# Top-k attention into a Sinkhorn mixture of experts: order of weight conversions, output copies and block boarding

## The chip, the cores and the metric

One core of one Trainium2 chip. The metric is the device time of one execution in microseconds (us). TensorE (PE in the profile) multiplies, VectorE (DVE), ScalarE (ACT) and GpSimd (POOL) do the rest, and the queue of SyncE (SP) issues the transfers.

## The reference

Attention over 4 batches of 8 heads, 576 tokens, head size 64, in which each query keeps only its 32 highest scores; its output, 2304 tokens of 512 features, goes through 8 dense experts whose outputs are summed with weights that a Sinkhorn iteration balances.

```python
def _attn_ref(q, k, v):                       # q, k, v: (4, 8, 576, 64)
    scores = scale * np.matmul(q, k.transpose(0, 1, 3, 2))
    kth = np.partition(scores, -top_k, axis=-1)[..., -top_k:-top_k + 1]   # top_k = 32
    scores = np.where(scores >= kth, scores, -1000000000.0)
    attn = np.exp(scores - np.max(scores, axis=-1, keepdims=True))
    attn = attn / (np.sum(attn, axis=-1, keepdims=True) + 1e-09)
    return np.matmul(attn, v)

def _moe_ref(x, w_gate, w1, w2):              # x: (2304, 512), w1: (8, 512, 1024), w2: (8, 1024, 512)
    logits = x @ w_gate
    P = np.exp(logits - logits.max())
    for _ in range(8):
        P /= P.sum(1, keepdims=True) + 1e-09
        P /= P.sum(0, keepdims=True) + 1e-09
        P *= N / E
    for e in range(E):
        h = np.maximum(x @ w1[e], 0.0)
        out += P[:, e:e + 1] * (h @ w2[e])
```

## The kernel before, in words

**Precision.** Most products are made from a high and a low part of each factor (`wh`, `wl` of a weight; `xh`, `xl` of the tokens; `hh`, `hl` of the hidden layer), as three matmuls. Splitting a weight tile of 128 x 1024 is a *conversion*: a transfer into `wr` (3 buffers), ACT's copy to `wh` (line 81, `hi_act`) and POOL's subtraction to `wl` (line 87, `lo_pool`), with 6 buffers each for `wh` and `wl`.

**Attention.** It runs in seven stages; a stage is a batch and one or two phases of 256 queries. A phase goes through four head pairs. For each score tile PE multiplies (lines 122 and 123, 4 matmuls), ACT copies (`s`, line 131, 3 buffers), and DVE finds the 32 highest by four MAX (line 142) and three MATCH_REPLACE (line 147) passes over 576 columns. ACT makes the exponentials and scales them, PE transposes (line 239, 9 transposes for two score tiles), ACT and DVE (or POOL, `evac_pool`, in the very first phase) split the result, PE multiplies by v (lines 252 and 253), and DVE adds the two halves into `xt` (line 256), a quarter of it for each head pair. Where both halves exist the four head pairs give `xt`, 256 tokens ("a block").

**Visits.** The MoE hides under the attention. Blocks 0, 1, 2, 3 and 5 are *boarded* into two seats of 256 columns: ACT and DVE split `xt` into the seat's `xh` and `xl` (lines 367 and 368). Then turn v, a call of `visit`, takes expert v mod 8 to every block that is seated, and a block leaves after 8 turns. The table `BOARD` names the turn at which a block boards; there are 24 turns. In a turn the hidden layer comes first (line 424, into p1), then `store_hidden` (lines 473 and 474), then the second product (line 511), whose result ACT copies to `y` (line 519) for a transfer to memory. If both seats are taken (and neither by block 0), one matmul of 512 columns serves both; a block alone has matmuls of 256 columns.

Block 0 is special. `first_half` multiplies its first two quarters with half of every expert's `w1` in plain float32 while the last two head pairs are still in work (lines 454, 457, 459: matmul, copy, transfer to memory); the visit adds the stored half (line 469) and needs only the other half of `w1`, so a turn with block 0 alone converts 6 tiles and others 8.

**The rest.** The four blocks that never board are multiplied at the end by one level of Strassen's scheme (`hidden_pair`, `last_outputs`), from factors that ACT and POOL make when the attention is over.

**What sets the order.** Each engine runs its instructions in a fixed order. A scheduler sets it when the program is built: of what is ready in its own reckoning, the highest priority goes first. Attention stages have priority BIG, `store_hidden` 2 BIG, `first_half` -BIG, everything else of a visit none. Attention stages are emitted when their `xt` buffers (3) are free, which hangs on `BOARD`.

Of the kernel before, what the change touches and what calls it, by code (L numbers as in the profile page):

```python
# [9 lines left out]
AF = mybir.ActivationFunctionType  # L10
# [4 lines left out]
DM, E, F = 512, 8, 1024  # L15
N = NB * S
NT = N // 128
KD = DM // 128
# [14 lines left out]
BLOCKS.append([("m", 0, 1), ("m", 2, 3)])  # L33


BOARD = {0: 0, 1: 4, 2: 8, 3: 12, 5: 16}
SEAT = {0: 0, 1: 1, 2: 0, 3: 1, 5: 0}


# [10 lines left out]
def kernel(  # L50
# [11 lines left out]
    nc = tc.nc  # L62
    BIG = 1000000
# [237 lines left out]
    def attend_stage(b, phases, mix):  # L301
        xts = {}
        for ph in phases:
            xts[ph] = xp.tile([128, KD, 256], F32, name="xt", bufs=XR)
            for t in range(2):
                X["t", b, 2 * ph + t] = xts[ph][:, :, t * 128:(t + 1) * 128]
        xm = None
        if mix:
            m = ("m", b // 2 * 2, b // 2 * 2 + 1)
            if m not in X:  # L310
                X[m] = xp.tile([128, KD, 128], F32, name="xm", bufs=2)
                mixed[m] = 0
            xm = X[m][:, :, (b % 2) * 64:(b % 2) * 64 + 64]
            mixed[m] += 1
        for hp in range(HP):
            if (b, phases, hp) == (0, (0,), 2):
                with tc.high_priority(offset=-BIG):
                    first_half(xts[0])
            attend_heads(b, hp, phases, xts, xm)
        for ph in phases:  # L320
            t = tile_id["t", b, 2 * ph]
            if 2 * b + ph == PARKED:
                nc.sync.dma_start(parked, xts[ph])
            gate_logits(xts[ph], [t, t + 1])
        if mix and mixed[m] == 2:
            gate_logits(X[m], [tile_id[m]])
# [77 lines left out]
    def convert(src, shape):  # L404
        wr = wp.tile(shape, F32, name="wr", bufs=WR)
        nc.sync.dma_start(wr, src)
        return split_weights(wr, shape)

    def split_weights(wr, shape):
        wh = wp.tile(shape, F32R, name="wh", bufs=WB)  # L410
        wl = wp.tile(shape, F32R, name="wl", bufs=WB)
        hi_act(wh, wr)
        lo_pool(wl, wr, wh)
        return wh, wl
# [13 lines left out]
    def hidden(seat, n, s, wh, wl):  # L428
        m = 512 // n
        for f0 in range(0, 2, m):  # L430
            ps = ps1.tile([128, m, n], F32, name="p1")
            products(ps, f0, seat, n, wh, wl, 0)
            with tc.high_priority(offset=2 * BIG):
                store_hidden(seat, slice(2 * s + f0, 2 * s + f0 + m), slice(seat.c0, seat.c0 + n), ps)
# [5 lines left out]
    def half_weights(e, s2, half):  # L440
        wr = wp.tile([128, 2, 2, 256], F32, name="wr", bufs=WR)
        for r in range(2):
            nc.sync.dma_start(wr[:, r], w1[e, 2 * s2 + r, :, 2 * half:2 * half + 2, :])
        return wr

    def first_half(x):
        for e in range(E):
            for s2 in range(2):
                wr = half_weights(e, s2, 0)
                for r in range(2):  # L450
                    ps = ps1.tile([128, 2, 256], F32, name="p1")
                    for fo in range(2):
                        for kk in range(2):
                            nc.tensor.matmul(ps[:, fo, :], wr[:, r, kk, fo * 128:(fo + 1) * 128], x[:, kk, :],  # L454
                                             start=(kk == 0), stop=(kk == 1))
                    y = op_.tile([128, 512], F32, name="y", bufs=YB)
                    nc.scalar.activation(y, ps.rearrange("p a b -> p (a b)"), AF.Copy)
                    PART[e, 2 * s2 + r] = dram.tile([128, 512], F32, name=f"p{e}_{s2}_{r}")
                    nc.sync.dma_start(PART[e, 2 * s2 + r], y)

    def second_half(e, s, seat, wh, wl, k0):
        y = op_.tile([128, 512], F32, name="y", bufs=YB)
        nc.sync.dma_start(y, PART[e, s])
        y = y.rearrange("p (a b) -> p a b", a=2)
        ps = ps1.tile([128, 2, 256], F32, name="p1")
        products(ps, 0, seat, 256, wh, wl, k0)
        ft = slice(2 * s, 2 * s + 2)
        with tc.high_priority(offset=2 * BIG):
            nc.vector.tensor_tensor(ps, ps, y, op=OP.add)
            store_hidden(seat, ft, slice(0, 256), ps)  # L470

    def store_hidden(seat, ft, cs, src):
        nc.scalar.activation(seat.hh[:, ft, cs], src, AF.Relu)  # L473
        nc.vector.scalar_tensor_tensor(seat.hl[:, ft, cs], src, 0.0, seat.hh[:, ft, cs].bitcast(F32),  # L474
                                       op0=OP.max, op1=OP.subtract)

    def visit(v, on):
        e = v % E
        ids = [SEAT[blk] for blk in on]
        groups = []  # L480
        if on[0] == 0:
            on_first, ids = True, ids[1:]
        else:
            on_first = False
        if 0 in ids and 1 in ids:
            groups, ids = [(seats[0], 512)], [i for i in ids if i > 1]
        groups += [(seats[i], 256) for i in ids]
        if groups:
            for s in range(4):
                wh, wl = convert(w1[e, s], [128, KD, 256])  # L490
                if on_first:
                    second_half(e, s, seats[0], wh[:, 2:4], wl[:, 2:4], 2)
                for seat, n in groups:
                    hidden(seat, n, s, wh, wl)
        else:
            for s2 in range(2):
                wr = half_weights(e, s2, 1)
                wh, wl = split_weights(wr, [128, 2, 2, 256])
                for r in range(2):
                    second_half(e, 2 * s2 + r, seats[0], wh[:, r], wl[:, r], 2)  # L500
        ws = [convert(w2[e, s], [128, 2, 512]) for s in range(4)]
        for blk in on:
            seat = seats[SEAT[blk]]
            for ti, piece in enumerate(BLOCKS[blk]):
                ts = slice(seat.c0 + ti * 128, seat.c0 + (ti + 1) * 128)
                ps = ps2.tile([128, 512], F32, name="p2")
                i = 0
                for ft in range(NFT):
                    wh, wl = ws[ft // 2]
                    for a, m in ((seat.hh, wh), (seat.hh, wl), (seat.hl, wh)):  # L510
                        nc.tensor.matmul(ps, a[:, ft, ts], m[:, ft % 2, :],  # L511
                                         start=(i == 0), stop=(i == 3 * NFT - 1))
                        i += 1
                output(v, tile_id[piece], ps)

    def output(v, t, ps):
        e = v % E
        y = op_.tile([128, 512], F32, name="y", bufs=YB)
        nc.scalar.activation(y, ps, AF.Copy)
        spill[t, e] = dram.tile([128, 512], F32, name=f"y{t}_{e}")  # L520
        nc.sync.dma_start(spill[t, e], y)

# [264 lines left out]
```

## Time and profile before

| | |
|---|---|
| median of 3 runs | 1947.8 us (1945.65 to 1948.59) |
| profiled execution, its own time | 1946.94 us |
| its span in the trace | 1945.2 us |
| PE busy | 1874.1 us, 96% |
| DVE busy | 1351.9 us, 70% |
| ACT busy | 1145.8 us, 59% |
| POOL busy | 1057.5 us, 54% |
| TensorE clock granted, mean | 0.989 |

The span is the time from the first to the last instruction that the trace holds; 1.7 us of the execution lie around it. Busy shares are means over stages with different limits: until about 476 us DVE is busy nearly all the time, from there PE is. All times below are from this one execution.

### The profile page before, as it was taken

How to read it: one execution, taken by the hardware profiler on the slowest of the kernel's cores; microseconds unless marked ns; L12 is line 12 of the kernel's file. 1: busy time of each engine (PE TensorE's matmuls, PEld its weight loads, DVE VectorE, ACT ScalarE, POOL GpSimd, SP SyncE). 2: the span in 40 equal slices, each digit the busy share in tenths (PEclk: the TensorE clock that was granted, in tenths of full speed). 3: DMA queues.
4: the chain of work that ended last, by engine and by line, in shares of the span. 5: the costliest groups of instructions: out<-in, count | busy, mean ns of one | idle time of the engine just before them, and what ended most of it. 6: DMA issues, size and time to landing. Idle time of an engine off the chain costs nothing.

```text
span 1945.2 us, 27297 instructions
## 1 busy us (share of the span) xinstructions
PE 1874.1 (96%) x9617; PEld 1590.8 (82%) x9617; DVE 1351.9 (70%) x2620; ACT 1145.8 (59%) x1993; POOL 1057.5 (54%) x914
## 2 busy tenths in 40 slices
PE   4799889999999999999999999999999999999998
PEld 3688788998888888888888888888888888888886
DVE  8979999999988998469998823135555555543333
ACT  6978877777777787568777754543333333333331
POOL 4548866645645445464444478864545544555440
PEclk9899989999999999999999999999999999999999
DMA  3477654434434324343333325633333333311211
GB/s 117 135 240 263 212 173 159 141 123 148 127 118 129 111 89 143 119 153 119 99 113 111 98 87 174 206 129 98 103 113 114 105 113 103 92 60 55 65 33 43
DMA packets 96073, 240.02 MB, mean 123 GB/s; under 512 B 10816, under 2 KB 12992, under 8 KB 95936
## 3 DMA queue, kind: packets, MB, share of 16 engines
q1 hardware_dynamic: 95936, 238.28, 38.4%
q8 instruction: 75, 1.23, 0.3%
q14 instruction: 62, 0.51, 0.1%
HBM read 203.64 MB, written 34.60 MB: 122 GB/s over the span
## 4 chain that ended last, share of the span: by engine, by line
PE 82%; DVE 12%; DMA 2%; ACT 1%; issue 1%; POOL 1%; SPq 0%; ACTq 0%; POOLq 0%; DVEq 0%
PE p L511 18%; PE p L681 18%; PE p L424 18%; PE p L622 9%; DVE m L142 5%; PE pc L622 5%; DVE w L147 4%; PE pb L622 2%; PE pt L239 2%; PE p L454 2%; PE sp L123 2%; PE sp L122 2%; PE pt L252 2%; PE pt L253 2%; DVE hl L474 1%
## 5 line engine op out<-in xcount | busy, mean ns | idle before, releaser
L87 POOL TENSOR_TENSOR wl<-wr,wh 128x1024 fp32r<-128x1024 f32 x280 | 675.7, 2424 | 520.0 <-ACT wh L81 504.1
L81 ACT ACTIVATE wh<-wr 128x1024 fp32r<-128x1024 f32 x280 | 296.2, 1060 | 297.8 <-PE p L622 194.4
L142 DVE MAX8 m<-w 128x8 f32<-128x576 f32 x432 | 318.6, 749 | 2.9
L424 PE MATMUL p<-xh,wh 128*128 128x256 f32 (+1 forms) x768 | 263.6, 343 | 6.7 <-DVE hl L474 6.7
L424 PE MATMUL p<-xl,wh 128*128 128x256 f32 (+1 forms) x768 | 261.4, 341 | 1.7 <-DVE xl L90 1.7
L424 PE MATMUL p<-xh,wl 128*128 128x256 f32 (+1 forms) x768 | 262.1, 342 | 0.0
L511 PE MATMUL p<-wh,hh 128*128 128x512 f32 x640 | 253.1, 400 | 2.1 <-ACT hh L473 2.0
L511 PE MATMUL p<-wl,hh 128*128 128x512 f32 x640 | 251.9, 396 | 0.0
L511 PE MATMUL p<-wh,hl 128*128 128x512 f32 x640 | 245.8, 395 | 0.0
L147 DVE MATCH_REPLACE8 w<-m,w 128x576 f32<-128x576 f32 x288 | 213.3, 741 | 0.1
L528 DVE SCALAR_TENSOR_TENSOR acc<-p,P,acc 128x512 f32<-128x512 f32 x120 | 89.5, 750 | 166.8 <-PE p L681 166.8
L681 PE MATMUL p<-wh,h2h 128*128 128x512 f32 x512 | 200.0, 391 | 1.3 <-ACT h2h L645 0.7
L681 PE MATMUL p<-wl,h2h 128*128 128x512 f32 x512 | 199.9, 390 | 0.0
L681 PE MATMUL p<-wh,h2l 128*128 128x512 f32 x512 | 196.7, 390 | 0.0
L474 DVE SCALAR_TENSOR_TENSOR hl<-p,hh 128x512 fp32r<-128x512 f32 x160 | 109.0, 682 | 100.0 <-ACT hh L473 99.0
L424 PEld LDWEIGHTS p<-xh,wh 128*128 128x128 f32 x768 | 146.7, 191 | 23.1 <-DVE hl L474 7.2
L424 PEld LDWEIGHTS p<-xl,wh 128*128 128x128 f32 x768 | 146.8, 191 | 16.9 <-DVE xl L90 2.0
L424 PEld LDWEIGHTS p<-xh,wl 128*128 128x128 f32 x768 | 146.7, 191 | 14.1
L142 DVE MAX8 m<-s 128x8 f32<-128x576 f32 x144 | 107.9, 749 | 50.6 <-ACT s L131 25.8
L511 PEld LDWEIGHTS p<-wh,hh 128*128 128x128 f32 x640 | 121.3, 190 | 23.2 <-ACT hh L473 2.4
L511 PEld LDWEIGHTS p<-wl,hh 128*128 128x128 f32 x640 | 121.5, 190 | 21.8
L511 PEld LDWEIGHTS p<-wh,hl 128*128 128x128 f32 x640 | 120.6, 189 | 22.6
(175 smaller groups left out, 4079.9 us busy)
## 6 DMA issues: line engine op xcount, KB each, us to landing
wr<-in_w_dram SPq DMA_DIRECT2D x240, 512.0 KB, 3.5
y<-y SPq DMA_DIRECT2D x160, 256.0 KB, 2.7
raw<-in_k_dram SPq DMA_DIRECT2D x56, 288.0 KB, 3.0
wr<-in_w_dram SPq DMA_DIRECT2D x48, 256.0 KB, 3.7
raw<-in_q_dram SPq DMA_DIRECT2D x32, 256.0 KB, 3.2
p<-y SPq DMA_DIRECT2D x32, 256.0 KB, 3.4
y<-p SPq DMA_DIRECT2D x32, 256.0 KB, 4.4
raw<-in_v_dram SPq DMA_DIRECT2D x28, 288.0 KB, 3.4
```

Of the source, the lines that this page charges most:

```text
L81: nc.scalar.activation(dst, src, AF.Copy)
L87: nc.gpsimd.tensor_tensor(dst, src, hi.bitcast(F32), op=OP.subtract)
L122: nc.tensor.matmul(o, qc, kh[:, cs], start=(i == 0), stop=False)
L123: nc.tensor.matmul(o, qc, kl[:, cs], start=False, stop=(i == n - 1))
L142: nc.vector.max(m8[:, u, r, :], ws[u] if r else units[u][0])
L147: nc.vector.match_replace(ws[u], m8[:, u, r, :], ws[u] if r else units[u][0], LOWEST)
L424: nc.tensor.matmul(ps[:, fo, :], a[:, kk, fs], x[:, k0 + kk, cs], start=(i == 0), stop=(i == 3 * nk - 1))
L474: nc.vector.scalar_tensor_tensor(seat.hl[:, ft, cs], src, 0.0, seat.hh[:, ft, cs].bitcast(F32), op0=OP.max, op1=OP.subtract)
L511: nc.tensor.matmul(ps, a[:, ft, ts], m[:, ft % 2, :], start=(i == 0), stop=(i == 3 * NFT - 1))
L528: return nc.vector.scalar_tensor_tensor(ACC[t], y, g, ACC[t], op0=OP.mult, op1=OP.add)
L622: nc.tensor.matmul(ps, w[:, kk, :], x[:, kk, :], start=(fresh and i == 0), stop=(i == 5), skip_group_check=True)
L681: nc.tensor.matmul(ps, a[:, ft, ts], m[:, ft, :], start=(i == 0), stop=(i == 11))
```

## The change

Three things. `BOARD` moves block 1 from turn 4 to turn 6 and block 3 from turn 12 to turn 14; the number of turns stays 24. The conversions of a visit are taken out of its loop into `visit_weights` and given priority 2 BIG, above attention, and so is the copy of an output (`y`, now line 530). And the conversions of the very first visit (two halves of `w1`, four tiles of `w2`) are called in stage one ahead of `first_half`, instead of at the visit.

```diff
--- before.py
+++ after.py
@@ -33,7 +33,7 @@
 BLOCKS.append([("m", 0, 1), ("m", 2, 3)])
 
 
-BOARD = {0: 0, 1: 4, 2: 8, 3: 12, 5: 16}
+BOARD = {0: 0, 1: 6, 2: 8, 3: 14, 5: 16}
 SEAT = {0: 0, 1: 1, 2: 0, 3: 1, 5: 0}
 
 
@@ -315,6 +315,7 @@
         for hp in range(HP):
             if (b, phases, hp) == (0, (0,), 2):
                 with tc.high_priority(offset=-BIG):
+                    ready[0] = visit_weights(0, True)
                     first_half(xts[0])
             attend_heads(b, hp, phases, xts, xm)
         for ph in phases:
@@ -474,6 +475,19 @@
         nc.vector.scalar_tensor_tensor(seat.hl[:, ft, cs], src, 0.0, seat.hh[:, ft, cs].bitcast(F32),
                                        op0=OP.max, op1=OP.subtract)
 
+    ready = {}
+
+    def visit_weights(v, alone):
+        e = v % E
+        if alone:
+            w1s = []
+            for s2 in range(2):
+                wh, wl = split_weights(half_weights(e, s2, 1), [128, 2, 2, 256])
+                w1s += [(wh[:, r], wl[:, r]) for r in range(2)]
+        else:
+            w1s = [convert(w1[e, s], [128, KD, 256]) for s in range(4)]
+        return w1s, [convert(w2[e, s], [128, 2, 512]) for s in range(4)]
+
     def visit(v, on):
         e = v % E
         ids = [SEAT[blk] for blk in on]
@@ -485,20 +499,16 @@
         if 0 in ids and 1 in ids:
             groups, ids = [(seats[0], 512)], [i for i in ids if i > 1]
         groups += [(seats[i], 256) for i in ids]
-        if groups:
-            for s in range(4):
-                wh, wl = convert(w1[e, s], [128, KD, 256])
-                if on_first:
-                    second_half(e, s, seats[0], wh[:, 2:4], wl[:, 2:4], 2)
-                for seat, n in groups:
-                    hidden(seat, n, s, wh, wl)
-        else:
-            for s2 in range(2):
-                wr = half_weights(e, s2, 1)
-                wh, wl = split_weights(wr, [128, 2, 2, 256])
-                for r in range(2):
-                    second_half(e, 2 * s2 + r, seats[0], wh[:, r], wl[:, r], 2)
-        ws = [convert(w2[e, s], [128, 2, 512]) for s in range(4)]
+        if v not in ready:
+            with tc.high_priority(offset=2 * BIG):
+                ready[v] = visit_weights(v, not groups)
+        w1s, ws = ready.pop(v)
+        for s, (wh, wl) in enumerate(w1s):
+            if on_first:
+                k0 = 2 if groups else 0
+                second_half(e, s, seats[0], wh[:, k0:k0 + 2], wl[:, k0:k0 + 2], 2)
+            for seat, n in groups:
+                hidden(seat, n, s, wh, wl)
         for blk in on:
             seat = seats[SEAT[blk]]
             for ti, piece in enumerate(BLOCKS[blk]):
@@ -516,7 +526,8 @@
     def output(v, t, ps):
         e = v % E
         y = op_.tile([128, 512], F32, name="y", bufs=YB)
-        nc.scalar.activation(y, ps, AF.Copy)
+        with tc.high_priority(offset=2 * BIG):
+            nc.scalar.activation(y, ps, AF.Copy)
         spill[t, e] = dram.tile([128, 512], F32, name=f"y{t}_{e}")
         nc.sync.dma_start(spill[t, e], y)
```

**Start of the program, ACT.** The rows are ACT's from its first splits of q and k on, before; `s` is the copy of a score tile, names with numbers are buffers.

```order
L81 ACTIVATE qs_105<-raw_103 128x512
L81 ACTIVATE kh_110<-raw_108 128x576
L81 ACTIVATE kh_116<-raw_114 128x576
L131 ACTIVATE s_139<-sp_134 128x576
L131 ACTIVATE s_146<-sp_141 128x576
L81 ACTIVATE qs_299<-raw_297 128x512
L81 ACTIVATE kh_304<-raw_302 128x576
L131 ACTIVATE s_208<-sp_203 128x576
L81 ACTIVATE kh_310<-raw_308 128x576
```

The same place of ACT in the changed kernel.

```order
L81 ACTIVATE qs_105<-raw_103 128x512
L81 ACTIVATE kh_110<-raw_108 128x576
L81 ACTIVATE kh_116<-raw_114 128x576
L81 ACTIVATE wh_494<-wr_491 128x1024
L131 ACTIVATE s_139<-sp_134 128x576
L81 ACTIVATE qs_299<-raw_297 128x512
L131 ACTIVATE s_146<-sp_141 128x576
L81 ACTIVATE wh_501<-wr_498 128x1024
L81 ACTIVATE kh_304<-raw_302 128x576
L131 ACTIVATE s_208<-sp_203 128x576
L81 ACTIVATE wh_507<-wr_505 128x1024
L81 ACTIVATE wh_513<-wr_511 128x1024
```

Six conversions (`wh`) of the first visit now stand among the first attention instructions, the first of them ahead of the first copy of scores; before, they stood after the 24th to 27th copy of scores.

**Second head pair of the first phase, DVE.** The rows are DVE's around the two additions that complete the second quarter of block 0's `xt` (`pt_465`, `pt_478`), which `first_half` needs; before.

```order
L142 MAX m8_1068<-s_1064 128x8
L147 MATCH_REPLACE w_1066<-m8_1068,w_1066 128x576
L148 SCALAR_TENSOR_TENSOR eb_945<-m8_943,nb_944 128x2
L256 TENSOR_TENSOR xt_102<-pt_465,tmp_464 64x256
L147 MATCH_REPLACE w_1067<-m8_1068,s_1064 128x576
L142 MAX m8_1068<-w_1066 128x8
L256 TENSOR_TENSOR xt_102<-pt_478,tmp_464 64x256
L142 MAX m8_1137<-s_1126 128x8
L142 MAX m8_1068<-w_1067 128x8
```

The same two additions in the changed kernel.

```order
L147 MATCH_REPLACE w_1173<-m8_1175,s_1164 128x576
L156 RECIPROCAL st_964<-st_964 128x2
L142 MAX m8_1106<-w_1105 128x8
L142 MAX m8_1175<-w_1173 128x8
L256 TENSOR_TENSOR xt_102<-pt_465,tmp_464 64x256
L256 TENSOR_TENSOR xt_102<-pt_478,tmp_464 64x256
L147 MATCH_REPLACE w_1105<-m8_1106,w_1105 128x576
L147 MATCH_REPLACE w_1173<-m8_1175,w_1173 128x576
```

Ahead of the second of them stood 52 MAX and 39 MATCH_REPLACE of DVE's order; now 57 and 42 do.

## Rows read from the trace of the kernel before

**Rows 1.** Busy time by stretch: length, busy (count) per engine, PEclk, DMA share, GB/s.

```profile
core 0: us, PE busy (x) PEld busy (x) DVE busy (x) ACT busy (x) POOL busy (x), PEclk, DMA share, GB/s
0.00:50.00 50.00, 22.52 (x75) 17.01 (x76) 44.47 (x93) 32.22 (x58) 21.11 (x34) 1.00 0.37 113
50.00:77.70 27.70, 18.12 (x78) 14.53 (x78) 27.54 (x60) 24.36 (x50) 18.01 (x30) 0.82 0.19 53
77.70:157.50 79.80, 75.59 (x406) 66.57 (x405) 63.25 (x137) 65.63 (x132) 35.40 (x48) 0.98 0.75 246
157.50:209.00 51.50, 47.74 (x304) 42.28 (x302) 50.39 (x102) 44.85 (x77) 49.00 (x42) 1.00 0.75 253
209.00:265.00 56.00, 48.28 (x275) 42.78 (x276) 55.03 (x106) 45.92 (x84) 43.13 (x40) 0.88 0.64 200
265.00:476.00 211.00, 201.64 (x1324) 184.47 (x1323) 205.04 (x433) 163.57 (x301) 122.85 (x131) 0.98 0.46 148
476.00:1276.00 800.00, 797.18 (x4287) 683.00 (x4287) 593.68 (x1263) 549.88 (x981) 451.30 (x379) 1.00 0.39 124
1276.00:1945.20 669.20, 663.08 (x2880) 540.13 (x2878) 312.50 (x432) 219.32 (x317) 316.66 (x214) 1.00 0.28 88
```

**Rows 2.** Timeline of PE: start us, length, operation, [idle before <-what ended it].

```profile
77.31 0.55 PE L239 MATMUL pt<-idt,Et 128*128 128x128 f32 x3 [0.77 <-DVE xt L256]
77.70 2.75 PE L454 MATMUL p<-xt,wr 128*128 128x256 f32 x12
...
152.26 2.88 PE L454 MATMUL p<-xt,wr 128*128 128x256 f32 x8 [2.75 <-ACT y L457]
...
265.12 0.28 PE L424 MATMUL p<-xh,wh 128*128 128x256 f32 x1
...
476.27 0.39 PE L424 MATMUL p<-xh,wh 128*128 128x512 f32 x1
```

**Rows 3.** Timeline of ACT, two places.

```profile
6.79 0.65 ACT L131 ACTIVATE s<-sp 128x576 f32<-128x576 f32 x1 [0.89 <-PE sp L123]
...
150.66 1.06 ACT L81 ACTIVATE wh<-wr 128x1024 fp32r<-128x1024 f32 x1 [2.75 <-DMA wr<-in_w_dram]
```

**Rows 4.** Timeline of DVE, three places.

```profile
101.17 0.74 DVE L142 MAX8 m<-w 128x8 f32<-128x576 f32 x1
101.83 0.07 DVE L147 MATCH_VALUE_LOAD w<-m,s 128x8 f32 x1
...
102.55 0.07 DVE L147 MATCH_VALUE_LOAD w<-m,w 128x8 f32 x1
...
117.35 0.76 DVE L142 MAX8 m<-s 128x8 f32<-128x576 f32 x1 [7.55 <-ACT s L131]
...
152.62 0.56 DVE L90 TENSOR_TENSOR atl<-pt,ath 128x384 fp32r<-128x384 f32 x1 [2.65 <-ACT ath L81]
```

**Rows 5.** The chain that ended last, in order of time: start us, us, what.

```profile
510.33 2.73 PE p L424 x12
...
1194.07 2.88 PE p L424 x24
```

**Rows 6.** The page's costliest groups: operation xcount | busy, mean ns | idle before.

```profile
L87 POOL TENSOR_TENSOR wl<-wr,wh 128x1024 fp32r<-128x1024 f32 x280 | 675.7, 2424 | 520.0 <-ACT wh L81 504.1
```

**Rows 7.** Groups of DVE between 265 and 476 us.

```profile
L474 DVE SCALAR_TENSOR_TENSOR hl<-p,hh 128x512 fp32r<-128x512 f32 x33 | 22.5, 680 | 2.1 <-ACT hh L473 2.0
...
L469 DVE TENSOR_TENSOR p<-p,y 128x512 f32<-128x512 f32 x16 | 11.0, 688 | 0.5 <-PE p L424 0.4
```

**Rows 8.** Line 148: duration ns min/median/max, first and last start us.

```profile
L148 DVE SCALAR_TENSOR_TENSOR eb<-m,nb x80: 132/230/2396, 22.5 to 1111.5; 128x2 f32<-128x2 f32 x64, 128x1 f32<-128x1 f32 x16
```

**Rows 9.** Timeline of the SP queue at the start.

```profile
3.07 0.91 SPq L443 DMA_DIRECT2D wr<-in_w_dram  x2
```

**Rows 10.** The page's transfers: xcount, KB each, median us from issue to landing.

```profile
wr<-in_w_dram SPq DMA_DIRECT2D x48, 256.0 KB, 3.7
```

**Rows 11.** Timelines of DVE and POOL: the last addition of attention, the last Strassen factor.

```profile
1143.66 0.22 DVE L258 TENSOR_TENSOR xm<-pt,tmp 64x64 f32<-64x64 f32 x1
...
1176.54 2.46 POOL L87 TENSOR_TENSOR T4l<-tf,T4h 128x1024 fp32r<-128x1024 f32 x1
```

## The prediction

> **What bounds the kernel now.** I read the busy time by stretch first, because a mean over the span hides that the limit changes. From 1276.0 us on the last four blocks run, PE is busy 663.08 of 669.20 us, and the change touches nothing there [rows 1]. From 476 to 1276 PE is busy 797.18 of 800 us: work taken from PE there is worth its full length, and a shorter wait of another engine is worth nothing. From 0 to 77.7 and from 157.5 to 476 DVE is busy nearly all the time (27.54 of 27.70, 50.39 of 51.50, 55.03 of 56.00, 205.04 of 211.00), while PE idles 27.5, 9.6, 3.8, 7.7 and 9.4 us in the five stretches; these are attention's stretches, whose length DVE's top-k passes set. Between 77.7 and 157.5 it is the other way round: PE works off `first_half`, idles 4.2 us, and DVE idles 16.6 us.
>
> Then the timelines, for what ended the idle times. `first_half` gets going at 77.70, right behind a DVE addition into `xt` [rows 2]. It ends late because of one wait: ACT stood 2.75 us for the transfer of a weight tile of the first visit [rows 3], the copy of PE's result stood behind it, and PE waited 2.75 us until 152.26 [rows 2]. DVE's two clear holes in the stretch, 7.55 and 2.65 us, end with ACT too [rows 4].
>
> **Part 1, boarding.** Turns 4 and 5 lose block 1 and turns 20 and 21 have two blocks instead of one, so paired turns go from 12 to 14. A hidden layer is 96 matmuls: 384 of 256 columns become 192 of 512. In the chain, 12 of 512 columns took 2.73 us and 24 of 256 took 2.88 us [rows 5], 0.228 and 0.120 each: 46.1 us become 43.8, 2.3 less. Half of it falls behind 476 us, where PE is the limit: **-1.1**. The other half is in part 2. Two more turns with block 0 alone mean four conversions fewer, at 2.42 us of POOL each [rows 6]. Behind 476 us POOL works 451 of 800 us [rows 1], so that is hidden; it would be worth 9.7 us at most if POOL were the limit.
>
> **Part 2, what the early turns now hold.** I counted PE's whole order. When turn 4 begins, both kernels have issued 147 transposes; before, 282 at the start of turn 8; changed, 246 at the start of turn 8 and the same 282 at the start of turn 9. So the same attention and (but for 1.2 us) the same visits lie between, distributed differently. Before, that took 265.12 to 476.27, 211.2 us [rows 2], with 205.0 us of DVE, of which visits have 22.5 + 11.0 = 33.5 [rows 7]: attention 171.5 for 135 transposes, 1.27 each. PE had 201.6, of it visits 4 x (144 x 0.120 + 96 x 0.228) = 156.7: attention 44.9, 0.333 each. Changed, up to turn 8: DVE 99 x 1.27 + 27.3 (two turns of 4 additions and 4 stores, two with 4 more stores) = 153.1, at DVE's present share of 97% 157.5; PE 33.0 + 33.4 + 78.3 = 144.7. DVE is the limit: 157.5. Turn 8: PE 43.8 + 36 x 0.333 = 55.8, DVE 51.1. PE is the limit. Together 213.3: **+2.1**. The work is the same but no longer evenly spread, which is where the small loss is from. From below 0 (the waits are filled), from above 6 (the 9.4 us that PE idles now are lost on top in equal share).
>
> **Part 3, the first visit's conversions in stage one.** Removed: ACT's wait of 2.75 us and with it PE's, **-2.75**; from below 0, since another copy may stand behind a transfer, from above 4.2, all that PE idled in the stretch. Added is work in the first 40 us: six conversions, 6 x 1.06 us of ACT [rows 3] and 6 x 2.42 = 14.5 us of POOL. ACT does 32.2 and POOL 21.1 of 50 us there [rows 1], so there is room; but what queues behind them is the chain that DVE lives on. Two steps. First, a `wh` now stands ahead of the first copy of scores. Its two transfers are issued from 3.07 us on [rows 9], the second some 0.48 later, and need 3.7 us [rows 10]: it starts at 7.2 and the copy, at 6.79 before [rows 3], at about 8.2: 1.4 us later, and all of DVE's top-k with it. Second, five MAX and three MATCH_REPLACE more stand ahead of the addition that `first_half` waits for. On DVE one MAX lasts 0.66 us from start to start and one MATCH_REPLACE with its load 0.72 [rows 4]: 5 x 0.66 + 3 x 0.72 = 5.5 us. DVE has no hole there to make that up. `first_half` gets going 6.9 us later, and everything behind it: **+6.9**. From below 1.4 (if the additions wait for their matmuls anyway and DVE's other holes shrink), from above 11.4, with two small DVE instructions blocked as follows.
>
> Line 148 is a DVE instruction on two columns. Its shortest took 132 ns, its longest 2396 [rows 8], about one POOL subtraction of 2424 ns [rows 6]. The Trainium skill, "SBUF - State Buffer", section "Who interferes with whom", says that a DVE instruction with both inputs in SBUF contends with a GpSimd instruction that reads SBUF, and that whoever issues first holds the shared pair for its whole length. The trace agrees with that length. By that rule alone each of the two or three such DVE instructions that meet the moved subtractions would cost up to 2.3 us, and none elsewhere; by the rows I take 0 for the likeliest and 2 x 2.3 for the upper bound, since the median is 230 ns.
>
> Between 157.5 and 209 POOL is busy 49.0 of 51.5 us [rows 1]; 14.5 us of that now lie earlier. DVE's holes from there to 265 are only 2.1 us, and the excess of line 148 is hidden in its busy time (0.23 less 0.13 us at the median, some 17 of them). I take **-1.2**, bounds 0 and -6.
>
> **Part 4, priority.** From turn 1 on the conversions stand between the same copies of scores as before, to within one or two, since they wait for one of six buffers anyway. PE waits nowhere by name for the output copy. So 0 here, and what hides a conversion is DVE's stock of three copied score tiles. If that cover is gone, the rival below is the price.
>
> **Sum.** -1.1 + 2.1 - 2.75 + 6.9 - 1.2 = +3.95. The profiled execution took 1946.94 us (span 1945.2 and 1.7 around it), 0.9 below the runs' median: **1950.9 us**.
>
> **Rivals.**
> 1. *Faster: DVE's holes close.* The first visit no longer disturbs ACT, and an earlier q load ends the wait of 7.55 us; then DVE, the limit from 157.5 to 476, has 7.55 + 2.65 us more. For it: both holes end with ACT, and ACT's own wait causes the second. Against it: PE's order gives out score tiles at the same pace, with `first_half` between them. With the late start made good (+6.9 becomes 0, the wait is inside the 10.2): 1946.9 - 1.1 + 2.1 - 10.2 - 1.2 = 1936.5. It decides from the point where the first visit's line 424 begins before 154 us.
> 2. *Slower: conversions starve attention.* Between 157.5 and turn 8 stand 46 conversions; where their `wh` or `wl` goes ahead of a small instruction that DVE waits for, it costs up to 1.06 or 2.42 us. At a quarter of the 1.06 each, 12 us: 1962.9. For it: DVE is the limit there, and ACT serves DVE in order. Against it: the conversions' places hardly moved. It decides from the point where DVE's share between 157.5 and turn 8 falls below 95%.
> 3. *Slower at the end.* Block 3's later boarding holds back the last attention stage, and the Strassen factors are late. Now the last addition is at 1143.66, the last factor at 1178.8 [rows 11], 97 us ahead of their use at 1276. Even two paired turns (2 x 43.8 us) would not use that up; if it did with 15 us on top, 1966.
>
> The Trainium skill would have rival 2 by way of the same shared pair: under the rule named above a higher priority for POOL's subtractions means more of them in flight when line 148 comes. No row tells the two ways apart.
>
> **How the numbers follow.** The likeliest case, 46 in 100, is the sum: 1944 to 1957 with its bounds. Rival 1 has 28, rival 2 21, rival 3 5. The range 1937 to 1963 leaves out some of rival 1, rival 3 and the outer part of rival 2. About 3.9 us (0.2%) is what a measurement can tell from no change. Faster than 1943.9: nearly all of rival 1 and a little of the likeliest, 0.30. Slower than 1951.7: rivals 2 and 3 and a quarter of the likeliest, 0.38. The rest 0.32.
>
> **What would show it.** The first MAX near 8.9 instead of 7.47 us; `first_half` going on near 84 us instead of 77.7; no wait of line 454 over 1 us; the first visit near 161 us instead of 157.5; turn 8 near 425 us, with PE idle some 13 us in the 160 before; PE without gaps from there; the last stretch 669 us as now. The prediction is wrong if DVE idles much less than 16 us ahead of the first visit, or much more than 3% behind it.

## The result, and the profile after

The changed kernel took 1969.9 us (median, 1967.65 to 1973.63), the kernel before 1946.7 in the same comparison: a ratio of 1.012, interval 1.0102 to 1.0139, 23 us slower. The forecast was 1950.9 with a range up to 1963. The profiled execution has a span of 1965.9 us against 1945.2 [rows 1], 20.7 longer; the account below is of these two.

The changed kernel by stretch, cut where its own stages begin: until `first_half` goes on, until the first visit, until turn 4, until turn 8, until turn 9, until the last visit's end, to the end (columns as in [rows 1]).

```profile
0.00:87.90 87.90, 41.74 (x150) 32.91 (x151) 78.97 (x167) 64.13 (x116) 54.45 (x71) 0.91 0.39 117
87.90:166.30 78.40, 76.10 (x406) 66.85 (x405) 55.43 (x120) 61.97 (x127) 29.93 (x45) 0.97 0.75 243
166.30:281.60 115.30, 99.36 (x588) 88.16 (x587) 113.21 (x217) 90.14 (x158) 83.63 (x79) 0.93 0.59 191
281.60:446.00 164.40, 146.59 (x937) 132.38 (x936) 159.64 (x316) 126.86 (x231) 101.06 (x103) 0.96 0.49 159
446.00:499.90 53.90, 53.90 (x279) 45.89 (x278) 52.54 (x109) 40.71 (x76) 30.57 (x30) 1.00 0.39 128
499.90:1296.60 796.70, 794.80 (x4195) 677.43 (x4195) 598.90 (x1264) 537.49 (x968) 428.63 (x369) 1.00 0.37 119
1296.60:1965.90 669.30, 663.17 (x2880) 540.16 (x2879) 313.28 (x432) 220.35 (x318) 319.67 (x215) 1.00 0.28 88
```

Read the lengths against those of before (77.7, 79.8, 107.6, 211.2 to the start of turn 8, which has the same attention behind it as turn 9 now, 799.7, 669.2): **+10.2, -1.4, +7.7, +7.1, -3.0, +0.1**, together the 20.7 by which the spans differ. All of the loss lies ahead of 500 us, where DVE sets the pace but for the stretch of `first_half`. DVE's idle time there is length less busy: 30.3 us before [rows 1], now 8.9 + 23.0 + 2.1 + 4.8 + 1.4 = 40.1. So 9.8 of the 23.6 us by which turn 9 is late are idle time of DVE, and 13.8 are busy time.

What the busy time is, two lines of DVE show: their groups up to turn 8 of the kernel before (xcount | busy, mean ns),

```profile
L148 DVE SCALAR_TENSOR_TENSOR eb<-m,nb 128x2 f32<-128x2 f32 x31 | 17.2, 556 | 0.1
L90 DVE TENSOR_TENSOR xl<-xt,xh 128x256 fp32r<-128x256 f32 x12 | 9.2, 769 | 0.0
L148 DVE SCALAR_TENSOR_TENSOR eb<-m,nb 128x1 f32<-128x1 f32 x3 | 0.7, 223 | 0.0
```

and up to turn 9 of the changed kernel:

```profile
L148 DVE SCALAR_TENSOR_TENSOR eb<-m,nb 128x2 f32<-128x2 f32 x31 | 27.7, 895 | 0.1
L90 DVE TENSOR_TENSOR xl<-xt,xh 128x256 fp32r<-128x256 f32 x12 | 10.7, 896 | 0.0
L148 DVE SCALAR_TENSOR_TENSOR eb<-m,nb 128x1 f32<-128x1 f32 x3 | 1.3, 428 | 0.1
```

The same 46 instructions take 39.7 us instead of 27.1: 12.6 of the 13.8. They do no more work; they are held, and by POOL's subtractions. In each kernel 17 of these 34 instructions of line 148 last over 0.33 us, and each of these 17 ends within 0.03 us of the end of a subtraction of line 87. It is not a wait for `nb`, which POOL makes for line 148 as well: each `nb` had been ready for at least 3.9 us. What the change altered is which subtraction they met: that of a weight (`wl`, the longest) 5 times before, 11 times now. DVE's timeline at two of the held instructions,

```profile
208.70 2.37 DVE L148 SCALAR_TENSOR_TENSOR eb<-m,nb 128x2 f32<-128x2 f32 x1
...
338.45 4.95 DVE L90 TENSOR_TENSOR xl<-xt,xh 128x256 fp32r<-128x256 f32 x1
```

and POOL's at the same places:

```profile
208.37 2.69 POOL L87 TENSOR_TENSOR wl<-wr,wh 128x1024 fp32r<-128x1024 f32 x1 [1.51 <-ACT wh L81]
...
338.34 1.02 POOL L87 TENSOR_TENSOR vz<-raw,vz 64x64 fp32r<-64x64 f32 x2
339.32 2.40 POOL L87 TENSOR_TENSOR wl<-wr,wh 128x1024 fp32r<-128x1024 f32 x1
341.68 1.43 POOL L87 TENSOR_TENSOR kl<-raw,kh 128x576 fp32r<-128x576 f32 x1
343.19 0.39 POOL L87 TENSOR_TENSOR vz<-raw,vz 64x64 fp32r<-64x64 f32 x1
```

The first DVE instruction ends at 211.07 us, POOL's subtraction at 211.06. The second ends at 343.40, 0.3 us behind the last of four subtractions that followed each other without a pause (338.34 to 343.11); that it got in only at POOL's pause is read from these times. The Trainium skill, "SBUF — State Buffer", section "Who interferes with whom", says that a DVE instruction with both inputs in SBUF contends with a GpSimd instruction that reads SBUF. The trace agrees, with 2.37 us for an instruction whose shortest is 132 ns [rows 8].

The start of the loss is in stage one. ACT's timeline, and DVE's (the first MAX, the second addition into `xt`, the longest hole):

```profile
7.71 1.06 ACT L81 ACTIVATE wh<-wr 128x1024 fp32r<-128x1024 f32 x1 [0.95 <-DMA wr<-in_w_dram]
8.67 0.63 ACT L131 ACTIVATE s<-sp 128x576 f32<-128x576 f32 x1
...
84.52 0.68 ACT L81 ACTIVATE kh<-raw 128x576 fp32r<-128x576 f32 x1 [1.88 <-DMA raw<-in_k_dram]
85.23 0.78 ACT L255 ACTIVATE tmp<-pt 64x256 f32<-64x256 f32 x2
```

```profile
9.33 0.76 DVE L142 MAX8 m<-s 128x8 f32<-128x576 f32 x1 [1.79 <-ACT s L131]
...
86.11 0.87 DVE L256 TENSOR_TENSOR xt<-pt,tmp 64x256 f32<-64x256 f32 x2
...
128.72 0.76 DVE L142 MAX8 m<-s 128x8 f32<-128x576 f32 x1 [9.85 <-ACT s L131]
```

The first MAX of the kernel before:

```profile
7.47 0.76 DVE L142 MAX8 m<-s 128x8 f32<-128x576 f32 x1 [0.78 <-ACT s L131]
```

The first MAX comes 1.86 us later than before. The two additions that `first_half` waits for start at 86.11, when DVE is through with the MAX ahead of them (86.08); the `kh` that waited 1.88 us for its load delayed their copy on ACT (`tmp`, done at 86.01), but by these times not the additions. In the stretch behind, DVE idles 23.0 us instead of 16.6; the longest hole is 9.85 instead of 7.55 us [rows 4]. By the first visit DVE has done about as many instructions as before (287, before 289), 8.8 us later. What it did more ahead of `first_half` (167, before 152) it lacks while PE, which sets the pace there, works `first_half` off.

### The profile page after: what moved, and what is told of

The parts are those of the page before. It is cut to its first block, busy times and chain, and to the rows that moved or that the text cites. A ratio compares the mean times of both kernels' runs of the same rounds, so it can differ in the third digit from the quotient of the medians.

```text
span 1965.9 us, 26901 instructions
## 1 busy us (share of the span) xinstructions
PE 1875.7 (95%) x9425; PEld 1583.8 (81%) x9425; DVE 1372.0 (70%) x2620; ACT 1141.6 (58%) x1989; POOL 1047.9 (53%) x910
## 4 chain that ended last, share of the span: by engine, by line
PE 76%; DVE 16%; DMA 3%; ACT 2%; issue 1%; POOL 1%; SPq 0%; POOLq 0%; ACTq 0%; DVEq 0%
PE p L692 18%; PE p L521 16%; PE p L425 16%; PE p L633 9%; DVE m L142 6%; DVE w L147 5%; PE pc L633 5%; PE pb L633 2%; PE pt L239 2%; PE p L455 2%; PE pt L253 1%; PE sp L123 1%; PE pt L252 1%; PE sp L122 1%; DVE eb L148 1%
## 5 line engine op out<-in xcount | busy, mean ns | idle before, releaser
L87 POOL TENSOR_TENSOR wl<-wr,wh 128x1024 fp32r<-128x1024 f32 x276 | 665.6, 2423 | 509.2 <-ACT wh L81 481.1
L81 ACT ACTIVATE wh<-wr 128x1024 fp32r<-128x1024 f32 x276 | 290.9, 1059 | 283.5 <-PE p L633 182.6
L425 PE MATMUL p<-xh,wh 128*128 128x512 f32 (+1 forms) x704 | 251.7, 358 | 4.8 <-DVE hl L475 4.8
L425 PE MATMUL p<-xh,wl 128*128 128x512 f32 (+1 forms) x704 | 250.3, 356 | 0.0
L425 PE MATMUL p<-xl,wh 128*128 128x512 f32 (+1 forms) x704 | 249.8, 355 | 0.0
L425 PEld LDWEIGHTS p<-xh,wh 128*128 128x128 f32 x704 | 134.1, 190 | 23.1 <-DVE hl L475 5.0
L425 PEld LDWEIGHTS p<-xl,wh 128*128 128x128 f32 x704 | 134.1, 190 | 16.8
L425 PEld LDWEIGHTS p<-xh,wl 128*128 128x128 f32 x704 | 133.9, 190 | 16.8 <-POOL wl L87 0.3
L142 DVE MAX8 m<-s 128x8 f32<-128x576 f32 x144 | 107.9, 749 | 50.5 <-ACT s L131 36.4
L521 PEld LDWEIGHTS p<-wh,hl 128*128 128x128 f32 x640 | 120.7, 189 | 24.4 <-DVE hl L475 2.1
```

The costliest lines, as they stand in the source:

```text
L81: nc.scalar.activation(dst, src, AF.Copy)
L87: nc.gpsimd.tensor_tensor(dst, src, hi.bitcast(F32), op=OP.subtract)
L142: nc.vector.max(m8[:, u, r, :], ws[u] if r else units[u][0])
L425: nc.tensor.matmul(ps[:, fo, :], a[:, kk, fs], x[:, k0 + kk, cs], start=(i == 0), stop=(i == 3 * nk - 1))
L521: nc.tensor.matmul(ps, a[:, ft, ts], m[:, ft % 2, :], start=(i == 0), stop=(i == 3 * NFT - 1))
```

## The experiments

Each time is the median and, in brackets, the ratio to the kernel before on the same chip with its interval. The table behind the experiments gives what the trace of most kernels says up to turn 9 (turn 8 with the old boarding). Each trace is of one execution, which can lie several us off the median.

**Boarding alone.**

```
-BOARD = {0: 0, 1: 4, 2: 8, 3: 12, 5: 16}
+BOARD = {0: 0, 1: 6, 2: 8, 3: 14, 5: 16}
```

> The kernel before with blocks 1 and 3 boarded two turns later and nothing else. Theory A (the loss is made by the conversions: in stage one they hold up the loads, in the turns POOL's subtractions hold up DVE): boarding is worth its own small sum, +1 us, between -2 and +4, so about 1948 us; line 148 and the low half of xt together stand no longer on DVE than before (15 us between 157 and 537 us). Theory B (the uneven early turns are what costs): +7 us or more, 1954 us, with PE idle over 20 us between the first visit and turn 8.

1944.7 us (0.9981, 0.9970 to 0.9993): a small gain, 3.7 us, just below theory A's range. Theory B is out.

**The first visit's conversions in stage one alone.**

```
                 with tc.high_priority(offset=-BIG):
+                    ready[0] = visit_weights(0, True)
                     first_half(xts[0])
```

> The kernel before with the first visit's six weight conversions written into stage one, at the priority of the first half, and no other priority; old boarding. (The conversions of a visit are also written ahead of its products, as in the changed kernel.) Theory A: the first MAX near 9.3 us, the first half of block 0 goes on near 86 us instead of 77.3, DVE idles over 20 us between there and the first visit, which begins near 166 us; in all +9 to +13 us, 1956 to 1960 us. Theory B: the late start is made up before the first visit or in the turns, within 4 us of the kernel before.

1961.6 us (1.0061, 1.0040 to 1.0083). Theory A's signs are all there: first MAX 9.02, `first_half` on at 87.7, 23.1 us of DVE idle behind it, first visit at 166.3 us.

**The conversions' priority alone**, none in stage one:

```
+            with tc.high_priority(offset=2 * BIG):
+                ready[v] = visit_weights(v, not groups)
```

> The kernel before with all visits' weight conversions (the first visit's too, but not moved into stage one) at the highest priority; old boarding, output copies as before. Theory A: the first visit begins near 157 us as before; from there to turn 9 DVE loses 8 to 12 us more than before in line 148 and in the low half of xt, each of which then ends within 0.03 us of a subtraction of POOL; in all +7 to +12 us, 1954 to 1959 us. Theory B: the conversions' places hardly move, within 4 us of the kernel before.

1944.1 us (0.9975, 0.9965 to 0.9985): faster than both kernels. Theory A was wrong: up to turn 8 the two lines take hardly more of DVE than before (28.4 us against 27.1). Where the gain is made stays open: the profiled execution, 1947.7 us, is the slowest of its ten.

**The output copies' priority alone.**

```
+        with tc.high_priority(offset=2 * BIG):
+            nc.scalar.activation(y, ps, AF.Copy)
```

> The kernel before with the output copies of the visits at the highest priority on ACT and nothing else. Both theories: nothing that is waited for moves, within 4 us of the kernel before. A third (C, the copies stand ahead of the copies of scores that DVE waits for): +4 us or more, with DVE's waits for the copied scores longer by as much between 157 and 476 us.

1951.1 us (1.0010, 1.0000 to 1.0021): nothing that matters.

The four parts give -3.7, +11.9, -4.9 and +1.9, together +5 us; the whole gives +23. So the parts meddle with each other, and the next experiments put them together or take one away.

**The changed kernel without stage one's part.**

```
-                    ready[0] = visit_weights(0, True)
```

> The changed kernel without the first visit's conversions in stage one: boarding, priority of the conversions and of the output copies stay. Theory A (the conversions in stage one are most of the loss, the rest adds to it as measured alone): -3.7 of boarding, -4.9 of the conversions' priority and +1.9 of the copies make -7, about 1940 to 1946 us where the kernel before is at 1947; first visit near 157 us. Theory B (the parts meddle with each other in the turns, without stage one): 1953 us or more, with line 148 and the low half of xt together over 30 us between the first visit and the time that attention of turn 9 is reached.

1955.7 us (1.0049, 1.0032 to 1.0066): Theory B by time. Stage one's part is worth 14 us here (1.012 against 1.0049), about what it costs alone; the other three together lose 9.5 us where alone they gain 7. The trace is of little help for this kernel: its profiled execution took 1951.7 us, the shortest of all its executions, which go up to 1961.3. The sign that theory B named, over 30 us on the two lines between the first visit and turn 9, is not in it (24.4 us).

**Boarding and the conversions' priority together.** (The two edits above.)

> Boarding two turns later and all conversions at the highest priority, nothing else. Theory A (what made boarding and priority together slower than either is these two): 1952 to 1958 us. Theory B (it was the output copies' priority on top of them): 1938 to 1945 us, the sum of the two gains.

1955.1 us (1.0038, 1.0023 to 1.0052): it is these two. The groups of the two lines between turn 4 and turn 9:

```profile
L148 DVE SCALAR_TENSOR_TENSOR eb<-m,nb 128x2 f32<-128x2 f32 x13 | 14.2, 1095 | 0.2
L90 DVE TENSOR_TENSOR xl<-xt,xh 128x256 fp32r<-128x256 f32 x4 | 4.5, 1134 | 0.0
L148 DVE SCALAR_TENSOR_TENSOR eb<-m,nb 128x1 f32<-128x1 f32 x3 | 1.9, 628 | 0.0
```

20.6 us; between turns 4 and 8 of the kernel before the same instructions took 9.4, and in the changed kernel 19.8. With one of the two parts alone the two lines stay below 30 us over the whole stretch up to the same point; with both they take 36.4 (table below).

**Line 148 off DVE.** The sum on two columns goes to ACT, the same values:

```
-        nc.vector.scalar_tensor_tensor(eb[:, 0:n], m8[:, 0:n, 3, 7], 0.125, nb[:, 0:n],
-                                       op0=OP.mult, op1=OP.add)
         for u, (s, Em, rsum) in enumerate(units):
+            nc.scalar.activation(eb[:, u:u + 1], m8[:, u, 3, 7:8], AF.Prelu, bias=nb[:, u:u + 1], scale=0.125, alpha=1.0)
```

In the changed kernel:

> The changed kernel with the two-column sum of line 148 taken from DVE to ACT (the same values; one ACT instruction a column), so that DVE has nothing with both inputs in SBUF there to be held by a subtraction of POOL. Between the first visit and 563 us line 148 takes 26 us of DVE in the changed kernel. Theory A (those are on the path, since DVE is the limit there): 15 to 22 us faster than the changed kernel, 1948 to 1955 us. Theory B (DVE would have waited anyway, or the wait moves to the low half of xt and to ACT): within 5 us of the changed kernel, 1965 to 1972 us.

1956.8 us (1.0045, 1.0027 to 1.0062), faster than the changed kernel by 13 us (medians) or 15 us (ratios): between the theories, nearer to A. The stretch up to turn 9:

```profile
0.00:489.00 489.00, 419.37 (x2359) 366.54 (x2360) 435.71 (x901) 396.62 (x773) 298.88 (x329) 0.94 0.54 172
```

DVE is busy 24.1 us less than in the changed kernel, idles 53.3 instead of 40.1, and turn 9 comes 10.9 earlier. So of the 31.9 us that the two lines no longer take, 10.9 come back by turn 9; 13.2 turned into idle time, and 7.8 went to other work of DVE that now lies ahead of turn 9. In the kernel before:

> The kernel before with line 148 on ACT in the same way. It takes 15.2 us of DVE there between 157 and 537 us, and 5 us before. Theory A: 8 to 18 us faster, 1929 to 1939 us. Theory B: within 4 us of the kernel before.

1944.6 us (0.9986, 0.9977 to 0.9996): Theory B. There the holding is no loss of its own; DVE idles 44.9 us instead of 30.3. This version has the second addition into `xt` 57 MAX down DVE's order, as the changed kernel does, without any conversion ahead of it; `first_half` goes on at 82.9 us, and the 5.2 us are made good by turn 8. To keep the addition at its old place (behind 52 MAX), the next one leaves the first six top-k on DVE (`if len(topks) <= 6`, with a count of the calls):

> The kernel before with line 148 on ACT only from the seventh top-k on, so that its first six stay on DVE and the second addition into xt keeps its place in DVE's order (behind 52 MAX and 39 MATCH_REPLACE, where the version with all on ACT had 57 and 44). Theory A (the place of that addition sets when the first half goes on, and later DVE idles what it was ahead): the first half goes on near 78 us as before instead of 83, DVE idles near 16 us ahead of the first visit instead of 24, and the time is 4 to 8 us below the version with all on ACT, 1936 to 1941 us. Theory B (the place doesn't matter, DVE makes it up): within 3 us of the version with all on ACT, 1942 to 1948 us.

1948.8 us (1.0005, 0.9991 to 1.0019): Theory A is out, and theory B is missed by a little, since the time is 4 us above the version with all on ACT. `first_half` goes on at 78.6 us, but that is worth nothing, and DVE idles 20.3 us behind it. So with line 148 on ACT a late `first_half` costs nothing by itself. The same with priority, and with the other parts:

> The same with all visits' conversions at the highest priority as well (none in stage one; old boarding). Theory A: 3 to 6 us below the version without priority, as the priority alone was worth 4.9 us: 1931 to 1938 us. Theory B (the priority's gain was that subtractions stood elsewhere when line 148 came, and is gone with line 148): the same as without priority, 1936 to 1941 us.

1943.2 us (0.9979, 0.9967 to 0.9991), above both theories' ranges and no better than the priority alone.

> The kernel before with three things: boarding two turns later, conversions at the highest priority (none in stage one), line 148 on ACT; output copies as before. Theory A: -3.7, -4.9 and -8 to -18 add up, 1920 to 1932 us, faster than both kernels. Theory B: about -8, 1939 us.

1957.0 us (1.0044, 1.0029 to 1.0059): both theories wrong; boarding and priority lose together here too. The two lines take 8.7 us up to turn 9 instead of 36.4, DVE idles 50.4 instead of 35.5, and turn 9 begins at 486.1 instead of 486.6. So with hardly any holding of line 148 left these two lose as much as with it (1.0038).

> Boarding two turns later, all conversions at the highest priority, and line 148 on ACT from the seventh top-k on. Theory A (the two together lose because subtractions of POOL hold line 148 and the low half of xt 10 us longer between turns 4 and 9): 8 to 14 us below boarding and priority without it, 1941 to 1947 us, DVE held under 6 us between turns 4 and 9 instead of 16.8. Theory B (DVE then waits for PE or ACT as long): within 4 us of it, 1951 to 1958 us, with DVE's idle time there longer by what the holding is shorter.

1952.6 us (1.0019, 1.0006 to 1.0032), 4 us below the two without it: Theory B by time. The two lines take 23.9 us less than without it (12.5 us), but DVE idles only 7.6 us more (43.1).

> Boarding two turns later with line 148 on ACT from the seventh top-k on, no priority. Theory A: DVE is held 9.7 us between turns 4 and 9 with boarding alone; some 5 us come back, 1938 to 1943 us. Theory B: as boarding alone, 1943 to 1948 us.

1959.8 us (1.0063, 1.0048 to 1.0078), by the ratios 16 us above boarding alone: neither theory. DVE idles 48.9 us up to turn 9. With line 148 on ACT from the seventh top-k on, then, it is boarding alone that loses, 11 us against the version without it (1.0063 and 1.0005), and the priority takes 9 of them back (1.0019): which parts meddle with each other changes with the place of a sum on two columns.

**One pair instead of six conversions in stage one.**

```
-                    ready[0] = visit_weights(0, True)
+                    first_pair()
```

> The kernel before with only the first of the first visit's six conversions in stage one, the other five at their place in the visit; no priority, old boarding. Theory A (the bulk of the six costs, by POOL's time in stage one and by the five MAX and five MATCH_REPLACE more that then stand ahead of the second addition into xt): here that addition stands behind 52 and 40, so the first half goes on near 80 us and the time is 1 to 4 us above the kernel before, 1949 to 1952 us. Theory B (the one conversion ahead of the first copy of scores costs most of it): 1956 us or more.

1958.3 us (1.0054, 1.0038 to 1.0070): Theory B by time. The pair's `wh` stands ahead of the first copy of scores, as with all six:

```profile
7.58 1.06 ACT L81 ACTIVATE wh<-wr 128x1024 fp32r<-128x1024 f32 x1 [1.08 <-DMA wr<-in_w_dram]
8.54 0.63 ACT L131 ACTIVATE s<-sp 128x576 f32<-128x576 f32 x1
```

But it doesn't cost there. `first_half` goes on at 80.1, the first visit begins at 152.6, 5 us earlier than before, and then come turns 0 to 3:

```profile
80.10:152.60 72.50, 70.56 (x381) 62.26 (x380) 55.29 (x118) 58.06 (x118) 33.54 (x46) 1.00 0.79 257
152.60:271.60 119.00, 102.10 (x604) 90.81 (x603) 113.04 (x224) 99.13 (x173) 91.18 (x84) 0.91 0.62 208
```

119.0 us instead of 107.6: DVE had done 19 instructions less in the stretch ahead of the visit (118 against the 137 of [rows 1]) and idles 6.0 instead of 2.1 us behind. That the early first visit is paid for by the attention that it overtakes is a reading of this trace and no rule: in the next version it begins at 153.2, and turns 0 to 3 take 109.0.

**The first visit's conversions behind `first_half`**, with priority:

```
                     first_half(xts[0])
+                    ready[0] = visit_weights(0, True)
```

> All conversions at the highest priority, old boarding, and the first visit's conversions written right behind the first half of block 0 instead of ahead of it, so that none stands in stage one. Theory A: the second addition into xt keeps its place (52 MAX, 39 MATCH_REPLACE), the first half goes on near 78 us, and the time is that of the priority alone, 1940 to 1947 us. Theory B (any conversion of the first visit ahead of its turn holds up the stage): 1952 us or more.

1958.6 us (1.0044, 1.0029 to 1.0059), Theory B by time: the addition keeps its place and `first_half` goes on at 77.6, but by the ratios the time is 13 us above the priority alone. The profiled execution, 1952.5 us, is one of its shortest, with the loss behind turn 8 (804.5 us to the last visit's end instead of 799.7). Its cause stays open.

**A control.** All versions with early conversions or with the conversions' priority also write a visit's conversions ahead of its products. That alone, without priority:

> A control: the kernel before with each visit's conversions only written ahead of its products, as the changed kernel and the versions with early conversions have them, with no priority, none in stage one, old boarding. Theory A (conversions in stage one cost 10 to 12 us by themselves): within 4 us of the kernel before. Theory B (any new order of ACT, POOL and DVE costs this kernel some 10 us, and the early ones were charged with it): 1955 us or more.

1950.8 us (1.0019, 1.0004 to 1.0034): Theory A. If the two simply add, some 4 of the 12 us are from the order in which the code is written and the other 8 from the conversions in stage one; and by the ratios the priority by itself gains some 9 us against this control.

What the traces say up to turn 9 (turn 8 with the old boarding), in us: when it begins; DVE's idle time, which is that less DVE's busy time in the stretch; and the two lines (line 148, and line 90 into `xl`).

| kernel | turn begins | DVE idle | two lines |
|---|---|---|---|
| before | 476.3 | 30.3 | 27.1 |
| conversions' priority | 479.2 | 33.0 | 28.4 |
| boarding | 480.1 | 36.1 | 29.8 |
| output copies' priority | 478.6 | 31.2 | 30.2 |
| written ahead | 483.3 | 33.3 | 28.7 |
| one pair early | 483.6 | 40.6 | 25.2 |
| boarding and priority | 486.6 | 35.5 | 36.4 |
| six conversions early | 489.9 | 40.4 | 30.0 |
| changed | 499.9 | 40.1 | 39.7 |
| changed, line 148 on ACT | 489.0 | 53.3 | 7.8 |
| before, line 148 on ACT | 476.6 | 44.9 | 9.3 |
| boarding and priority, line 148 on ACT | 486.1 | 50.4 | 8.7 |
| boarding and priority, line 148 on ACT from the seventh | 483.1 | 43.1 | 12.5 |
| boarding, line 148 on ACT from the seventh | 488.0 | 48.9 | 13.4 |

Without the last two columns every row is between 414 and 428 us: DVE's other work changes little, in part because not quite the same attention lies ahead of the cut (276 to 288 transposes). Early conversions show in the idle column, boarding with priority in the last one, and the changed kernel has both. Where line 148 is on ACT the last column empties and the idle column fills. One column alone does not tell the time: the output copies' priority has 30.2 us on the two lines, 3.1 more than before, and takes 2 us more.

## Why the prediction was wrong, point by point

Of the 20.7 us the sum had 3.95. The step that failed is the one that put the holding of DVE's two-input instructions at nothing: part 3 takes "0 for the likeliest", and part 4 says "So 0 here". In its place these instructions took 12.6 us more of DVE up to turn 9. Behind the first visit it is 2.8 of the +7.7 and 10.4 of the +7.1 us, in stretches where DVE idles as much as before (2.1 and 6.2 us, before 2.1 and 6.0). A second term was mis-sized, the delay of `first_half` (+6.9, measured +10.2). And the sum took its parts as independent, where the four parts alone give +5 and the whole +23.

- **Boarding, -1.1 and +2.1.** No loss alone, but not the sum either (+1.0 forecast, -3.7 measured, interval -5.8 to -1.4). The 2.1 was reckoned with DVE's work per transpose as before; in the changed kernel that stretch is +7.1, since line 148 and `xl` take 10.4 us more in it. The part behind turn 9 gave -3.0, in the direction forecast.
- **ACT's wait removed, -2.75.** The wait is gone (line 455 waits at most 0.7 us), but the stretch became only 1.4 us shorter.
- **`first_half` later, +6.9.** The mechanism was right, the size too small: +10.2. DVE idles 3.2 us more ahead of it, 1.86 of them by the later first MAX, where the sum had 1.4; and it is busy 7.0 us more, where the sum had 5.5 for eight top-k instructions and nothing for what came along with them.
- **"DVE has no hole there to make that up."** True, and not enough: behind it DVE idled 6.4 us more. The forecast said that the reading would be wrong if DVE idled much less than 16 us ahead of the first visit; it idled more.
- **POOL relieved, -1.2.** This term had the wrong sign. Turns 0 to 3 took +7.7: line 148 from 5.2 to 11.8 us, `xl` from 5.5 to 1.7; the other 4.9 us are nine DVE instructions more in the stretch (217 against 208).
- **Priority, 0, "the conversions' places hardly moved".** Here is why that step failed: it looked at the order within POOL and ACT, not at what runs on POOL at the moment that line 148 comes. The value taken for holding was "0 for the likeliest and 2 x 2.3 for the upper bound"; it measured 12.6 up to turn 9. The median of 230 ns, from which the 0 was taken, says nothing of a tail up to 2396. The kernel before already lost in this way: on two columns line 148 took 556 ns in the mean up to turn 8.
- **Rival 2** named the price of the slower side (1962.9), and the paragraph behind the rivals a second way to it, the shared pair. The traces tell the two ways apart: behind the first visit DVE idles as much as before, so it is not starved, but the two lines take more. The sign that rival 2 gave to look for was wrong: DVE's share between the first visit and turn 8 is 272.85 of 279.70 us, 98%, not below 95, since a held instruction counts as busy.
- **Rivals 1 and 3** did not happen: the first visit began at 166.3 us, and the last stretch is 669.3 us as before. (By [rows 11] the last Strassen factor ended at 1179.0 us, not 1178.8, which changes nothing.)

What is shown: stage one's conversions cost 12 to 14 us, some 4 of them perhaps by the order of writing; boarding with priority costs 7 to 10 where each alone gains; POOL's subtractions hold line 148, those of weights 11 times instead of 5; 13 to 15 us come back when line 148 leaves DVE in the changed kernel, against 3 in the kernel before. What is only argued: that the 12.6 us of holding are lost in full, and that boarding and priority together are what moves the subtractions in line 148's way. Against making this the whole cause stands that boarding with priority loses as much with line 148 on ACT. What stays open: by what those two lose then, why DVE idles more in every version with line 148 on ACT, and why the conversions written behind `first_half` lose 13 us. The priority alone, at 0.9975, beats both kernels.

## What to carry to other kernels

In a schedule where one engine is busy 97% of a stretch, the parts of a change don't add: measure each alone and each pair before the sum is believed. Read the longest duration of a small instruction, not its median, and look at what the neighbouring engine runs at that moment; busy time can be waiting. Work moved into an "idle" stretch is not free when it stands ahead of the first link of the chain that the busy engine lives on.

## What the runs showed of the hardware

A DVE subtraction with both inputs in SBUF, which takes 0.41 us where nothing holds it (mean of four between turns 4 and 8 of the kernel before), lasted 4.95 us: by the times above it was held not by one POOL instruction but by all four that followed each other without a pause. Line 148's 17 long instructions up to turn 9 each ended within 0.03 us of the end of a POOL subtraction, whichever of its subtractions that was. And nine executions of one program, the one with the first visit's conversions behind `first_half`, took 1949.0 to 1961.1 us.
